# A score tile in PSUM with chunk 3 to the left of chunk 0, and two mask products at its head instead of three

## The chip, the cores and the metric

The kernel runs on one core of a Trainium2 chip. Its engines work side by side, each through its own queue in program order: TensorE (PE for its products, PEld for the loads of their weights), VectorE (DVE), ScalarE (ACT), GpSimd (POOL), and SyncE (SP), which issues most of the DMAs. The metric is the device time of one execution in microseconds (us); the profile gives one execution of its own with a span, from the first to the last instruction of the program.

## What is computed

Causal attention over 8 batches of 12 heads (448 positions, 64 per head), and on its output a soft mixture of experts with 8 experts of 4 slots each.

```python
scores = scale * np.matmul(q, k.transpose(0, 1, 3, 2))
mask = np.triu(np.ones((seq, seq), dtype=bool), k=1)
scores = np.where(mask, -1000000000.0, scores)
scores = scores - np.max(scores, axis=-1, keepdims=True)
attn = np.exp(scores)
attn = attn / (np.sum(attn, axis=-1, keepdims=True) + 1e-09)
out = np.matmul(attn, v)
...
logits = x @ phi
...
return (c @ slot_out).astype(np.float32)
```

## The kernel before

**Tiles.** Work goes head by head, i from 0 to 95 (`NHD`), two heads to a pair p. The scores of a head are held transposed: keys on the 128 partitions, queries along the columns. The keys are cut into four chunks of 128, 128, 128 and 64. Because of the causal mask, chunk c only meets queries from 128c on, so the chunks have 448, 320, 192 and 64 columns, 1024 in all: a tile `s` of two PSUM banks, of which three exist. Where each chunk lies is set by `SC0` to `SC3` (line 49): chunks 1 and 2 fill the first bank (columns 0 to 511), chunk 0 begins the second bank at 512 and chunk 3 ends it at 960.

**Products of a tile.** The first 128 columns of a chunk (64 for chunk 3) lie on the diagonal and need the mask. It is put there by TensorE: the weights are an identity in bf16 (`identb`) and the moving operand is `tri`, zeros with large negative numbers where a key is later than a query. `scores1(i, part)` (line 211) issues one product: `"c3"` and `"c0"` write the mask for chunks 3 and 0 (64 and 128 columns), `"c12"` that for chunks 1 and 2 in one product of 256 columns, since both lie in one bank; `"k0"` to `"k3"` add keys times queries (`ks` as weights, `qd` as moving operand). Each bank's first product carries `start`. Later `scores2` (`"t0"` to `"t3"`, line 285) adds the correction of the rounding and the row maxima, with `k2` as weights and `r2` as moving operand. Every product is preceded by a load of its weights; the weights of k0, k1 and k2 have 128 columns, those of k3 only 64.

**Readers of a tile.** `max_evac` (line 242) copies chunk 0 with ScalarE to `mx`, `max_keys` takes the maximum with chunks 1 to 3 on VectorE, `max_spread` puts the maxima into `r2` on GpSimd, `exps` (line 296) turns all 1024 columns into `pt`, and `attv` (line 300) multiplies it with the values: for each block qc of 128 queries a product for every chunk c up to qc, in f32, which the compiler makes two passes of. For qc = 3 only 64 queries are left and the weights have 65 columns, with one column more than needed; the last column of `pt` (1024) is a zero kept for this. The last head has a fresh PSUM tile, and there 128 columns are taken for c below 3.

**Order.** Each engine's order is written out by hand in `ORDER` (line 42), one list for even and one for odd i, and nothing is reordered. In round i the list issues the first products of head i + 2 (c, k), the corrections of head i (t), the value products of head i - 1 (a), the maxima (x, mr, sp), the norms (n), the casts and differences of coming pairs (ck, cq, sk, sq, c2), and at its end one item of a plan: transposes, logits or dispatch of a batch. Heads 0 to 3 get their first products in a row from `scores1_all` (line 238) before the rounds proper; heads 4 to 95 get them by `ORDER`.

**Start and tail.** Before the first scores, GpSimd makes `ident` and `tri` (line 153 on), and TensorE runs warm-up products with them. After the last head the experts run: 64 loads of 768 KB of weights, 22 of which go to buffers that are there from the start, the others to buffers that become free when attention ends.

Of the kernel before, what the change touches and what calls it, by code (L numbers as in the profile page):

```python
# [11 lines left out]
BF16 = mybir.dt.bfloat16  # L12
AF = mybir.ActivationFunctionType
ALU = mybir.AluOpType
# [3 lines left out]
P = 128  # L18
NB, NH, S, HD = 8, 12, 448, 64
# [10 lines left out]
NEG = -float(2 ** 33)  # L30
NHD = 2 * NPAIR
# [8 lines left out]


ORDER = (
# [4 lines left out]
)  # L47

SC0, SC1, SC2, SC3 = 512, 0, 320, 960
CQ0 = (0, 128, 256, 384)  # L50
SCOL = (SC0, SC1, SC2, SC3)

# [27 lines left out]
def attention_soft_moe(ctx: ExitStack, tc: tile.TileContext, qk, va, phi, w1, w2, out):  # L80
    nc = _Core(tc)
    const = ctx.enter_context(tc.tile_pool(name="const", bufs=1, side="left"))
# [29 lines left out]
    def load_qk(p, a, hs=slice(0, 2)):  # L112
        if p < NPAIR:
            if hs.start == 0:

                st["raw", a, p] = (wres.tile([P, WN], F32, tag="w", name=f"qk{a}_{p}")[:, 0:2 * S]
                                   .rearrange("p (h s) -> p h s", h=2)
                                   if (p, a) in ((1, 0), (2, 1)) else
                                   raw.tile([P, 2, S], F32, tag="qk", name=f"qk{a}_{p}"))
            nc.sync.dma_start(out=st["raw", a, p][:, hs], in_=qk[p, :, a, hs])  # L120

    def loads_v(p, eng=nc.sync):
        if p < NPAIR:
            eng.dma_start(out=va_[p % 2], in_=va[p])
# [12 lines left out]
    def load_w(n):  # L137
        if n < len(order):
            m, e, h, u = order[n]
            t = wtiles[order[n]] = slot(n, f"w{n}")  # L140
            nc.sync.dma_start(out=t, in_=(w1 if m == 0 else w2)[e, h, :, WN * u:WN * u + WN])

    for hs in (slice(0, 1), slice(1, 2)):
# [10 lines left out]
    nc.gpsimd.memset(ident, 0.0)  # L154
    nc.gpsimd.affine_select(out=ident, in_=ident, compare_op=ALU.not_equal, fill=1.0,
                            base=0, pattern=[[-1, P]], channel_multiplier=1)
    tri = const.tile([P, P], BF16, name="tri")
    nc.gpsimd.memset(tri, 0.0)
    nc.gpsimd.affine_select(out=tri, in_=tri, compare_op=ALU.is_ge, fill=NEG,
                            base=0, pattern=[[1, P]], channel_multiplier=-1)  # L160

    ops = [[fix.tile([P, 2, S], F32R, name=f"{o}{i}") for o in ("qd", "ks")] for i in range(NR)]
    qd_, ks_ = ([t[k] for t in ops] for k in range(2))
# [47 lines left out]
    def scores1(i, part):  # L211
        if i >= NHD:
            return
        p, h = divmod(i, 2)
        ks, qd = ks_[p % NR], qd_[p % NR]
        if ("s", i) not in st:
            st["s", i] = ps_s.tile([P, 1024], F32, tag="s", name=f"s{i}")
            st["open"] = set()
        s = st["s", i]

        bank = part in ("c12", "k1", "k2")
        start = bank not in st["open"]
        st["open"].add(bank)
        if part[0] == "k":
            c = int(part[1])
            w, m = S - CQ0[c], min(P, S - P * c)
            nc.tensor.matmul(s[0:m, SCOL[c]:SCOL[c] + w], ks[:, h, P * c:P * c + m],
                             qd[:, h, CQ0[c]:S], start=start, stop=False, skip_group_check=True)
            return
        if part == "c12":  # L230
            o = s[:, SC1:SC1 + 2 * SC2].rearrange("p (a n) -> p a n", n=SC2)[:, :, 0:P]
            mask = tri.unsqueeze(1).to_broadcast([P, 2, P])
        else:
            w = P if part == "c0" else S - 3 * P
            o, mask = s[:, SCOL[int(part[1])]:SCOL[int(part[1])] + w], tri[:, 0:w]
        nc.tensor.matmul(o, identb, mask, start=start, stop=False, skip_group_check=True)

    def scores1_all(i):
        for part in ("c0", "k3", "c3", "c12", "k2", "k1", "k0"):
            scores1(i, part)  # L240

    def max_evac(i):
        if i < NHD:
            st["mx", i] = (xtp.tile([P, 512], F32, tag="xt", name="mx1", bufs=2)[:, 0:S] if i == 1
                           else mx_)
            nc.scalar.activation(out=st["mx", i], in_=st["s", i][:, SC0:SC0 + S], func=AF.Copy)
# [38 lines left out]
    def scores2(i, cs):  # L285
        if i >= NHD:
            return
        p, h = divmod(i, 2)
        s = st["s", i]
        k2, r2 = k2_[p % NR], r2_[p % NR]  # L290
        for c in cs:
            w, m = S - CQ0[c], min(P, S - P * c)
            nc.tensor.matmul(s[0:m, SCOL[c]:SCOL[c] + w], k2[:, h, P * c:P * c + m],
                             r2[:, h, CQ0[c]:S], start=False, stop=True, skip_group_check=True)

    def exps(i):
        if i < NHD:
            nc.scalar.activation(out=pt_[i % 2][:, 0:1024], in_=st.pop(("s", i)), func=AF.Exp, scale=SCALE)

    def attv(i, qcs, first):  # L300
        if not 0 <= i < NHD:
            return
        p, h = divmod(i, 2)
        pt, v, po = pt_[i % 2], va_[p % 2], st.get(("po", i), po0)
        for qc in qcs:
            for c in range(qc + 1):
                col = SCOL[c] + P * (qc - c)


                m = P if qc < 3 or i == NHD - 1 and c < 3 else 65  # L310
                nc.tensor.matmul(po[0:m, qc], pt[:, col:col + m], v[:, c, h],
                                 start=c == 0 and qc in first, stop=c == qc, skip_group_check=True)

# [94 lines left out]
    for b in range(NB):  # L408
        o, last = 12 * b, b == NB - 1
# [14 lines left out]
    for hs in (h0, h1):  # L424
# [3 lines left out]
        sub_q(0, hs)  # L428
    scores1_all(0)
    scores1_all(1)  # L430
    warm(START[1])
    max_evac(0)
# [47 lines left out]
    for i in range(NHD + 1):  # L480
        p, h = divmod(i, 2)
        if h:
            load_qk(p + 3, 1)
            if p + 1 < NPAIR - 1:
                loads_v(p + 1)
            load_qk(p + 3, 0)
            if p % 2 and nload < RES:
                load_w(nload)
                nload += 1
        if i == NHD - 3:  # L490

            loads_v(NPAIR - 1, nc.scalar)
        if i < 2:
            scores2(i, (1, 0, 2))
            if i:
                scores1_all(3)
                max_evac(3)
            scores2(i, (3,))
            exps(i)
            if i == 0:  # L500
                max_row(1, 0)
                max_row(1, 1)
                max_spread(1)
                sub_q(1, h1)

        qs = [int(n[1]) for n in ORDER[h] if n[0] == "a"]
        first = qs[:2] if qs[0] == 3 else qs[:1]
        for n in ORDER[h]:
            if i < 2 and (n in ("ev", "exp") or n[0] in "kt" or n in ("c0", "c3", "c12")):
                continue  # L510
            if i == 0 and n in ("mr0", "mr1", "sp"):
                continue
            if n[0] == "k" or n in ("c0", "c3", "c12"):
                scores1(i + 2, n)
            elif n[0] == "t":
                scores2(i, (int(n[1]),))
            elif n[0] == "a":
                attv(i - 1, (int(n[1]),), first)
            elif n[0] == "x":
                max_keys(i + 2, int(n[1]))  # L520
            elif n[0] == "n":
                norm(i - 1, int(n[1]))
            elif n in ("mr0", "mr1"):
                max_row(i + 1, int(n[2]))
            elif n == "ld":
                if i % 12 == 3 and i > 12:
                    logits_d(i // 12 - 1, lt)
            elif n == "plan":
                if later and i:
                    later.pop(0)()  # L530
                plan.get(i, int)()
            else:
                {"ev": lambda: max_evac(i + 2), "exp": lambda: exps(i), "sp": lambda: max_spread(i + 1),
                 "ck": lambda: cast_k(p + 2), "sk": lambda: sub_k(p + 2), "cq": lambda: cast_q(p + 2),
                 "c2": lambda: copy_k2(p + 1), "sq": lambda: sub_q(p + 2)}[n]()
        if i == NHD - 1:

            scs.close()
            pe = att.enter_context(tc.tile_pool(name="pe", bufs=1, space=PSUM, reuse_waits="tile"))
            ps = [pe.tile([P, 512], F32, name=f"e{k}") for k in range(6)]  # L540
            po = st["po", i] = ps[2][:, 0:NCH * VC].rearrange("p (c n) -> p c n", n=VC)
# [44 lines left out]
    for hf in range(2):  # L586
        tps = (po0 if hf == 0 else po).rearrange("p a b->p (a b)")[:, 0:3 * NSLOT]
        for c in range(3):
            o = 384 * hf + P * c
# [130 lines left out]
    n = NBUF  # L720
# [80 lines left out]
```

## Time and profile before

| What | Value |
|---|---|
| three runs | 461.10, 459.82, 461.09 us |
| median | 461.09 us |
| profiled execution, its own time | 459.88 us |
| its span | 458.2 us |
| mean granted TensorE clock | 0.978 |
| HBM read, written | 107.25 MB, 11.01 MB |
| mask products (`s<-tri,identb`) | 288, busy 39.7 us, mean 234 ns |
| weight loads of `identb` | 320, mean 99 ns |

The span has two stages. Attention reaches to about 358 us and holds the 96 heads, at about 3.6 us each; in it GpSimd, VectorE, ScalarE and TensorE all work, and the DMA engines are about 70% busy. The rest are the experts, with the DMA engines full until close to the end. Rows of the profile give an engine, an operation, `out<-in` by the program's names, the shape, and a duration. For TensorE a product's duration is its way through the array, part of which overlaps with the next, so the pace is read from the distance between starts. All operations show line 64, that of a helper that records the program order, so they are told apart by their tiles.

### The profile page before, as it was taken

The numbers are of one execution on the slowest core, as the hardware profiler recorded it, in microseconds if no ns is written. First come the engines' busy times: TensorE is split into PE (matmuls) and PEld (weight loads), VectorE is DVE, ScalarE is ACT, GpSimd is POOL, SyncE is SP. The second block draws the span as 40 slices with busy tenths as digits, with TensorE's granted clock in tenths as the row PEclk, the third lists the DMA queues.
The fourth block names the chain that finished last, engine by engine and source line by source line (L and its number), as shares of the span: only waits on it lengthen the run. The fifth ranks groups of instructions, "written<-read, shape, count | busy, mean of one in ns | idle before, by whom it ended". The sixth has DMA issues, their size and how long they took to land.

```text
span 458.2 us, 12014 instructions
## 1 busy us (share of the span) xinstructions
PE 424.9 (93%) x4581; PEld 362.3 (79%) x4581; DVE 348.9 (76%) x1044; ACT 329.9 (72%) x496; POOL 266.3 (58%) x215
## 2 busy tenths in 40 slices
PE   6899999999999999999999999999999998996660
PEld 3798999999899989998999999999989654542230
DVE  6988888888888898888888888888886467332350
ACT  6898899889888988897899789988975211342240
POOL 5888777777777777777778777777771000000000
PEclk9999999999999999999999999999999999999875
DMA  7477666676667765777666766667758999999997
GB/s 267 128 259 243 235 193 224 216 239 223 204 208 237 236 221 171 241 241 231 210 188 225 254 222 216 191 213 253 231 160 300 369 411 415 414 414 413 402 391 284
DMA packets 38201, 119.04 MB, mean 260 GB/s; under 512 B 4096, under 2 KB 11776, under 8 KB 38144
## 3 DMA queue, kind: packets, MB, share of 16 engines
q1 hardware_dynamic: 38000, 118.01, 75.6%
q8 instruction: 36, 0.59, 0.5%
q10 hardware_dynamic: 144, 0.27, 0.2%
q14 instruction: 21, 0.17, 0.1%
HBM read 107.25 MB, written 11.01 MB: 258 GB/s over the span
## 4 chain that ended last, share of the span: by engine, by line
PE 77%; DMA 11%; POOL 5%; ACT 1%; DVE 1%; issue 1%; SPq 0%; POOLq 0%; ACTq 0%
PE po L64 34%; PE s L64 24%; DMA w<-in_w_dram 10%; PE xt L64 4%; PE g L64 3%; PE hp L64 3%; POOL r L64 3%; PE sp L64 2%; PE rt L64 2%; PE pp L64 2%; POOL ks L64 1%; PE e L64 1%; PE so L64 1%; DMA qk<-in_qk_dram 1%; ACT ot L64 0%
## 5 line engine op out<-in xcount | busy, mean ns | idle before, releaser
L64 PE MATMUL po<-va,pt 128*128 128x65 f32 x1900 | 193.6, 250 | 0.1
L64 PEld LDWEIGHTS po<-va,pt 128*128 128x128 f32 x1900 | 190.5, 171 | 0.5 <-issue 0.3
L64 DVE TENSOR_TENSOR mx<-s,mx 128x320 f32<-128x320 f32 (+2 forms) x288 | 100.8, 350 | 31.4 <-ACT mx L64 27.9
L64 POOL TENSOR_TENSOR r<-qk,qd 64x896 fp32r<-64x896 f32 (+1 forms) x50 | 101.5, 2030 | 6.5 <-ACT qd L64 2.7
L64 POOL TENSOR_SCALAR_AFFINE_SELECT r<-mr 14x448 fp32r<-14x448 f32 x96 | 61.4, 640 | 73.2 <-DVE mr L64 72.8
L64 ACT ACTIVATE pt<-s 128x1024 f32<-128x1024 f32 x96 | 98.2, 1023 | 6.3 <-PE s L64 3.1
L64 POOL TENSOR_TENSOR ks<-qk,ks 64x896 fp32r<-64x896 f32 (+1 forms) x47 | 98.1, 2087 | 4.5 <-ACT ks L64 0.9
L64 PE MATMUL s<-r,k 128*128 128x320 f32 (+3 forms) x384 | 83.2, 298 | 2.3 <-POOL r L64 2.2
L64 ACT ACTIVATE mx<-s 128x448 f32<-128x448 f32 x96 | 52.5, 546 | 36.0 <-PE s L64 22.2
L64 PE MATMUL s<-qd,ks 128*128 128x448 f32 (+3 forms) x384 | 76.0, 308 | 1.6 <-ACT qd L64 1.6
L64 PEld LDWEIGHTS s<-r,k 128*128 128x128 f32 (+1 forms) x384 | 60.0, 176 | 6.4 <-POOL r L64 2.9
L64 DVE STREAM_TRANSPOSE mt<-mx 128x448 f32<-128x448 f32 x96 | 61.9, 645 | 3.3
L64 DVE TENSOR_REDUCE r<-mt 128x14 f32<-128x448 f32 x96 | 58.4, 609 | 0.1
L64 PEld LDWEIGHTS s<-qd,ks 128*128 128x128 f32 (+1 forms) x384 | 55.0, 180 | 3.1 <-ACT qd L64 2.3
L64 ACT ACTIVATE ks<-qk 128x896 fp32r<-128x896 f32 (+1 forms) x50 | 45.6, 914 | 2.5 <-DMA qk<-in_qk_dram 2.5
L64 ACT ACTIVATE k<-ks 64x896 fp32r<-64x896 f32 (+1 forms) x49 | 45.8, 935 | 1.1
L64 ACT ACTIVATE qd<-qk 128x896 fp32r<-128x896 f32 (+1 forms) x50 | 46.1, 923 | 0.4 <-DMA qk<-in_qk_dram 0.3
L64 PEld LDWEIGHTS <-identb 128*128 128x128 bf16 x320 | 28.1, 99 | 20.1 <-issue 15.8
L64 DVE TENSOR_TENSOR x<-po,sm 128x256 f32<-128x256 f32 x95 | 40.3, 424 | 3.3
L64 PE MATMUL s<-tri,identb 128*128 128x64 bf16 (+2 forms) x288 | 39.7, 234 | 0.2
L64 ACT ACTIVATE xts<-xt 128x512 f32<-128x512 f32 x47 | 28.1, 598 | 6.7 <-PE xt L64 4.4
L64 PE MATMUL so<-w,ht 128*32 128x384 f32 x256 | 24.9, 492 | 7.4 <-DMA w<-in_w_dram 5.6
(124 smaller groups left out, 396.2 us busy)
## 6 DMA issues: line engine op xcount, KB each, us to landing
w<-in_w_dram SPq DMA_DIRECT2D x64, 768.0 KB, 7.5
qk<-in_qk_dram SPq DMA_DIRECT2D x94, 448.0 KB, 3.5
va<-in_va_dram SPq DMA_DIRECT2D x47, 260.0 KB, 3.5
out_dram<-ot SPq DMA_DIRECT2D x28, 384.0 KB, 6.5
qk<-in_qk_dram SPq DMA_DIRECT2D x4, 224.0 KB, 3.3
va<-in_va_dram ACTq DMA_DIRECT2D x1, 260.0 KB, 5.4
phi<-in_phi_dram SPq DMA_DIRECT2D x2, 48.0 KB, 3.9
```

What stands on the lines that cost most here:

```text
L64: return self._tc.keep_in_program_order(op(*args, **kwargs))
```

## The change

Chunk 3 moves to the head of the second bank (512), and chunk 0 behind it (576). The two diagonals of that bank are then neighbours, and one product of 192 columns, `"c03"`, writes both masks. Its moving operand is the new `tri3`, whose first 64 columns are the mask of chunk 3 and whose last 128 are the `tri` of before; GpSimd makes it with one memset and two selects. In both lists `"c03"` and `"c12"` stand first, and `"k3"` follows them; before it was `"c3", "c0", "k3", "c12"`. The order of `scores1_all` becomes `"c03", "k3", "c12", ...`.

Since it is now chunk 0 that ends the tile, its block for qc = 3 uses the zero column of `pt`. For the last head the value products of qc = 3 run in the order c = 1, 0, 2, 3, and only that of c = 1 takes 128 columns.

```diff
 ORDER = (
-    ("c3", "c0", "k3", "c12", "k1", "k0", "k2", "t0", "t2", "ev", "x1", "t1", "a0", "a3", "t3", "ck",
+    ("c03", "c12", "k3", "k1", "k0", "k2", "t0", "t2", "ev", "x1", "t1", "a0", "a3", "t3", "ck",
...
-    ("c3", "c0", "k3", "c12", "k0", "k1", "k2", "ev", "t0", "t1", "t2", "a0", "x0", "t3", "a3", "exp", "mr0",
+    ("c03", "c12", "k3", "k0", "k1", "k2", "ev", "t0", "t1", "t2", "a0", "x0", "t3", "a3", "exp", "mr0",
...
-SC0, SC1, SC2, SC3 = 512, 0, 320, 960
+SC0, SC1, SC2, SC3 = 576, 0, 320, 512
...
-    tri = const.tile([P, P], BF16, name="tri")
-    nc.gpsimd.memset(tri, 0.0)
-    nc.gpsimd.affine_select(out=tri, in_=tri, compare_op=ALU.is_ge, fill=NEG,
-                            base=0, pattern=[[1, P]], channel_multiplier=-1)
+    tri3 = const.tile([P, 64 + P], BF16, name="tri")
+    tri = tri3[:, 64:64 + P]
+    nc.gpsimd.memset(tri3, 0.0)
+    for t, n in ((tri3[:, 0:64], 64), (tri, P)):
+        nc.gpsimd.affine_select(out=t, in_=t, compare_op=ALU.is_ge, fill=NEG,
+                                base=0, pattern=[[1, n]], channel_multiplier=-1)
...
         else:
-            w = P if part == "c0" else S - 3 * P
-            o, mask = s[:, SCOL[int(part[1])]:SCOL[int(part[1])] + w], tri[:, 0:w]
+            o, mask = s[:, SC3:SC3 + 64 + P], tri3
         nc.tensor.matmul(o, identb, mask, start=start, stop=False, skip_group_check=True)

     def scores1_all(i):
-        for part in ("c0", "k3", "c3", "c12", "k2", "k1", "k0"):
+        for part in ("c03", "k3", "c12", "k2", "k1", "k0"):
             scores1(i, part)
...
         for qc in qcs:
-            for c in range(qc + 1):
+            last = qc == 3 and i == NHD - 1
+            for c in (1, 0, 2, 3) if last else range(qc + 1):
                 col = SCOL[c] + P * (qc - c)
-                m = P if qc < 3 or i == NHD - 1 and c < 3 else 65
+                m = P if qc < 3 or last and c == 1 else 65
```

More of the change, by code (lines that the diff above doesn't have):

```diff
@@ L508, in attention_soft_moe @@
         for n in ORDER[h]:
-            if i < 2 and (n in ("ev", "exp") or n[0] in "kt" or n in ("c0", "c3", "c12")):
+            if i < 2 and (n in ("ev", "exp") or n[0] in "kt" or n in ("c03", "c12")):
                 continue
@@ L512, in attention_soft_moe @@
                 continue
-            if n[0] == "k" or n in ("c0", "c3", "c12"):
+            if n[0] == "k" or n in ("c03", "c12"):
                 scores1(i + 2, n)
```

## The prediction

> **What bounds the kernel now.** I read the page first, for the shares of the engines and of the chain that ended last.
>
> ```profile
> span 458.2 us, 12014 instructions
> PE 424.9 (93%) x4581; PEld 362.3 (79%) x4581; DVE 348.9 (76%) x1044; ACT 329.9 (72%) x496; POOL 266.3 (58%) x215
> PE 77%; DMA 11%; POOL 5%; ACT 1%; DVE 1%; issue 1%; SPq 0%; POOLq 0%; ACTq 0%
> PE po L64 34%; PE s L64 24%; DMA w<-in_w_dram 10%; PE xt L64 4%; PE g L64 3%; PE hp L64 3%; POOL r L64 3%; PE sp L64 2%; PE rt L64 2%; PE pp L64 2%; POOL ks L64 1%; PE e L64 1%; PE so L64 1%; DMA qk<-in_qk_dram 1%; ACT ot L64 0%
> ```
>
> TensorE carries 77% of the chain, and its score products (s) and value products (po) carry 58%. Busy PE alone proves little, since the ends of products are modelled. So next come the busy time by stage, the waits from 39.4 to 346 us, and two places of the chain of waits.
>
> ```profile
> 39.40:346.00 306.60, 306.60 (x3364) 286.14 (x3365) 268.38 (x814) 266.55 (x380) 233.91 (x172) 1.00 0.70 219
> 362.00:458.20 96.20, 70.05 (x775) 35.62 (x774) 40.47 (x116) 23.74 (x61) 0.00 (x0) 0.90 1.00 394
> PEld L64 <- issue: 13.1, 36, 0.6
> PEld s L64 <- issue: 1.2, 7, 0.2
> PEld s L64 <- POOL r L64: 0.7, 1, 0.7
> 35.32 2.10 POOL ks L64
> 38.74 0.59 POOL r L64
> 39.38 0.72 PE s L64 x3
> ```
>
> The columns of the first two rows are the stretch, its length, PE, PEld, DVE, ACT and POOL busy, the granted clock, the DMA share and GB/s. From 39.4 to 346 us the next busiest engine after TensorE (DVE, 268.38) has 38 us to spare, the clock is full, and TensorE waits for another engine for at most 1.2 + 0.7 us; the 13.1 us are treated with the rivals. Up to 39.38 the chain runs through POOL, whose r ends TensorE's last long wait. From 362 us the DMA engines are full: that tail begins when attention frees its buffers, so attention's delay moves it.
>
> **The price of a product is read from the order of weight loads and streams.** Here is one score tile (starts first, then durations).
>
> ```profile
> 204.10 0.21 PEld L64 LDWEIGHTS <-identb 128*128 128x128 bf16 x2
> 204.21 0.25 PE L64 MATMUL s<-tri,identb 128*128 128x64 bf16 x2
> 204.24 0.14 PEld L64 LDWEIGHTS s<-qd,ks 128*64 128x64 f32 x1
> 204.27 0.22 PE L64 MATMUL s<-qd,ks 128*64 128x64 f32 x1
> 204.33 0.10 PEld L64 LDWEIGHTS <-identb 128*128 128x128 bf16 x1
> 204.33 0.28 PE L64 MATMUL s<-tri,identb 128*128 128x256 bf16 x1
> 204.33 0.20 PEld L64 LDWEIGHTS s<-qd,ks 128*128 128x128 f32 x1
> 204.46 0.34 PEld L64 LDWEIGHTS s<-qd,ks 128*128 128x128 f32 x2
> 204.60 0.45 PE L64 MATMUL s<-qd,ks 128*128 128x448 f32 x2
> 204.80 0.25 PE L64 MATMUL s<-qd,ks 128*128 128x192 f32 x1
> 204.81 0.19 PEld L64 LDWEIGHTS s<-r,k 128*128 128x128 f32 x1
> 204.91 0.39 PEld L64 LDWEIGHTS s<-r,k 128*128 128x128 f32 x2
> 202.07 0.55 PEld L64 LDWEIGHTS po<-va,pt 128*65 128x65 f32 x8
> 202.60 1.20 PEld L64 LDWEIGHTS po<-va,pt 128*128 128x128 f32 x10
> 202.71 1.23 PE L64 MATMUL po<-va,pt 128*128 128x65 f32 x10
> 7.96 0.61 PE L64 MATMUL warm<-tri,identb 128*128 128x512 bf16 x2
> 7.96 0.82 PE L64 MATMUL warm<-tri,identb 128*128 128x512 bf16 x3
> ```
>
> Prices, worked out:
>
> - A bf16 stream: a third 512-column product adds 0.82 - 0.61 = 0.21 us, or 0.41 ns a column.
> - A score stream: k0 (448 columns) starts at 204.60 and k2 at 204.80: 0.20 us, or 0.45 ns a column.
> - A load of 128 f32 columns: ten loads start over 1.20 - 0.19 us, so (1.20 - 0.19) / 9 = 0.112 us. Their products stream only 65 columns (0.03 us) and still come 0.11 us apart, so here the loads set the pace.
> - A load of 65 columns: (0.55 - 0.14) / 7 = 0.059 us; I take it for 64 too.
>
> The order: one load runs ahead, no more. The second of the two loads at 204.46 (k2's) starts when the product before it does, at 204.60 (0.46 + 0.34 - 0.19 = 0.61), though the load before it was through at 204.57. The r load at 204.81 starts with k2's product, and the next at 204.91, when that 0.1 us load is through. So a load is hidden as far as the product ahead of it streams, and the rest is idle time.
>
> In this kernel the long mask product c12 (256 columns, 0.105 us) hides the 0.112 us load of the key product k1. From c3's start to k1's: k0 starts at 204.60, less k1's 320 columns (0.143 us) gives 204.46, which is also where k0's load begins. So **0.25 us** before.
>
> **The change part by part.**
>
> *The two mask products merged and moved.* c3 (64 columns) and c0 (128) become c03 (192 columns); one bf16 load and one product go from each of 96 tiles. Since c12 now follows at once, the order is c03, c12, k3, k1 (k0 on odd heads). c03 streams 192 x 0.41 = 0.079 us and hides c12's load; c12 streams 0.105 us and hides k3's load of 0.059 us. Then k3 streams its 64 columns (0.029 us) and has to cover the 128-column load of k1, which starts when k3 does: 0.112 us. So 0.079 + 0.105 + 0.112 = **0.296 us** from the first mask to k1, against 0.25: **+0.046 us a tile**. What is late next is k1 and all behind it, since TensorE takes its queue in order. The mask moved ahead of k3 waits for the same tile to come free as c03 just before it, so no new wait is added, and no DMA or other queue is moved.
>
> No row of before has a 64-column score product followed by a 128-column f32 load, so the bounds: below, the load is hidden wholly, 0.079 + 0.105 + 0.029 = 0.213 us, or -0.037 a tile; above, the load starts only when k3's stream has ended, as c12's did (k3 starts at 204.24 + 0.06 = 204.30, c12's load at 204.33), 0.029 later, or +0.075 a tile. I take +0.046, the rule of the po loads, which are the nearest rows: a 65-column f32 stream ahead of a 128-column f32 load.
>
> The queue speaks for the low bound in one text: the Trainium skill, "TensorE: Matmul & The Clock Gate", table at its head, gives TensorE a 64-deep window that pulls weight loads ahead of products in flight. Taken as many loads ahead, it would make this change a gain, and the rows at 204.46 and 204.81 speak against it.
>
> How many tiles count:
>
> ```profile
> L64 PE MATMUL s<-tri,identb 128*128 128x256 bf16 x85 | 24.3, 285 | 0.0
> 66.96 0.95 ACT L64 ACTIVATE k<-ks 64x896 fp32r<-64x896 f32 x1
> 68.03 0.50 PEld L64 LDWEIGHTS s<-r,k 128*128 128x128 f32 x3 [0.17 <-issue]
> ```
>
> Of the 96 tiles, 85 lie between 39.4 and 346 us: 85 x 0.046 = 3.9 us. The seven in ORDER before 39.4 I cost at nothing, because POOL sets the pace there and TensorE waits for it anyway; without that cover 7 x 0.046 = 0.3 us. Seven waits (1.2 us) are like the one at 68.03, where ACT's copy k ends at 66.96 + 0.95 = 67.91 and TensorE stands 0.17 us: the later scores use up 0.046 of each, 7 x 0.046 = -0.3 us.
>
> *Start.* POOL gets a wider memset and one more select ahead of the warm-up.
>
> ```profile
> 1.58 0.29 POOL L64 TENSOR_SCALAR_AFFINE_SELECT tri<-tri 128x128 bf16<-128x128 bf16 x1
> 4.75 0.13 PEld L64 LDWEIGHTS s<-qd,ks 128*64 128x64 f32 x1 [0.59 <-ACT qd L64]
> 7.11 0.53 ACT L64 ACTIVATE mx<-s 128x448 f32<-128x448 f32 x1
> ```
>
> Some 0.3 us, after which the first scores end near 6 us instead of 5.7, while their reader, the copy mx, starts at 7.11: 0, and 0.3 without that cover. The first four tiles keep k3 ahead of c12 and lose one product, at a time when DMA and POOL set the pace: 0.
>
> *Last head.* Two of its value products, two passes each, load 65 columns instead of 128.
>
> ```profile
> L64 PEld LDWEIGHTS e<-va,pt 128*128 128x128 f32 x18 | 2.2, 192 | 0.2 <-issue 0.2
> ```
>
> 4 x (0.112 - 0.059) = -0.21 us, behind which the full DMA tail stands: 0, or -0.2 if that cover is gone.
>
> *Sum:* 3.9 - 0.3 = **+3.6 us**. The profiled execution took 459.88 us, so 463.5 by it. The median of the runs is 461.09, as two of the three lie near 461.1 and one at 459.8; +3.6 on it is 464.7. I put down **464.3**.
>
> **The rivals.**
>
> 1. *The load waits for k3 to end* (+0.075 a tile). For it: the late load at 204.33. Against it: the same step from a 64-column score product to the po loads, where the load at 202.07 is not late.
>
> ```profile
> 202.01 0.14 PEld L64 LDWEIGHTS s<-r,k 128*64 128x64 f32 x1
> ```
>
> 202.01 + 0.06 = 202.07. Price: 85 x 0.075 = 6.4, less 0.5 for the seven waits, plus 0.3 for the tiles before 39.4: +6.2 on the median, 467.3. The Trainium skill, "TensorEngine Tiling (Array Packing)", Key Properties, says that a change of tiling mode drains TensorE. By that rule k3's 64 columns would cost this wait; the two rows disagree about it. Chance 0.14.
>
> 2. *Faster: the load is hidden.* If TensorE keeps more than one load ready, k1's load runs under c12 beside k3's (0.059 + 0.112 = 0.171 us against 0.079 + 0.105 streamed), and only the missing waits remain: 85 x -0.037 = -3.1 on the median, or 458.0. It decides as soon as 0.046 us of the load starts before k3 does. The loads at 204.46 and 204.81 speak against it. Chance 0.12.
>
> 3. *No change:* TensorE has slack that no view names. The 36 waits of 13.1 us in front of mask loads would be such slack in 36 tiles; I read them as loads held back by long streams ahead (the logits and dispatch products). With them as slack, and a load hidden in part in the rest, the time stays near 461. Against it: 1.2 + 0.7 us are all the waits that name an engine or a queue on score loads, and 3.9 are needed. Chance 0.12.
>
> **How the numbers follow.** The forecast has 0.62. About 0.3% (1.4 us) is what a measurement of this kernel tells from no change. Slower: 0.62 + 0.14 = 0.76; same 0.12; faster 0.12. The range takes in rival 1 up to 467.3, and stops below at 460.2, which leaves out rival 2 and a little of rival 3.
>
> **What would show it.** Right: one mask form of 192 columns x96; k1's product some 0.30 us after the first mask of its tile, with the load of k1 starting beside k3 and the next load 0.11 us later; the stretch of 85 tiles longer by 3 to 4 us, and the DMA tail moved by as much. Wrong: k1's load under c12 (rival 2), k1's load 0.03 us after k3's start (rival 1), or a stretch no longer than before (rival 3). I would also be wrong if the moved layout made the copies or the exponential dearer, which no row suggests.

## The result

| | before | changed |
|---|---|---|
| median of six runs each | 461.10 us | 465.46 us |
| lowest, highest | 459.66, 463.04 | 465.02, 466.93 |
| profiled execution, span | 459.88, 458.2 | 465.78, 464.1 |

The ratio is 1.0103, with a 95% interval of 1.0072 to 1.0133: slower by 0.7 to 1.3%, as forecast, with 464.3 predicted and 465.46 measured. The profiled executions of the first and the seventh run below took 1416.37 and 621.32 us, with TensorE at a slow pace throughout, so those two kernels were run again for their profiles.

First the page of the changed kernel, then its two stretches from the view by windows: from the c12 product of head 11 to that of head 95, and the rest. The columns are the stretch, its length, PE, PEld, DVE, ACT and POOL busy, the clock, the DMA share and GB/s.

```profile
span 464.1 us, 11824 instructions
PE 431.1 (93%) x4485; PEld 367.7 (79%) x4485; DVE 348.7 (75%) x1044; ACT 330.0 (71%) x496; POOL 266.4 (57%) x216
L64 PE MATMUL s<-tri,identb 128*128 128x192 bf16 x96 | 24.2, 252 | 0.2
L64 PEld LDWEIGHTS <-identb 128*128 128x128 bf16 x224 | 19.4, 102 | 21.4 <-issue 17.9 <-DVE identb L64 1.7
```

```profile
44.54:352.29 307.75, 307.61 (x3236) 287.71 (x3236) 265.44 (x806) 264.15 (x377) 230.85 (x170) 1.00 0.69 215
352.29:464.00 111.71, 85.09 (x938) 48.57 (x937) 48.32 (x143) 31.06 (x73) 1.28 (x2) 0.93 0.99 389
```

The same two stretches of the kernel before:

```profile
42.59:345.81 303.22, 303.22 (x3322) 283.04 (x3320) 265.69 (x806) 263.79 (x377) 230.87 (x170) 1.00 0.69 218
345.81:458.20 112.39, 85.89 (x939) 49.16 (x937) 48.39 (x143) 31.12 (x73) 1.28 (x2) 0.91 0.99 386
```

The change does what it says: 96 products of 192 columns, and 96 loads of `identb` fewer (224 instead of 320). With them TensorE takes **307.75 us instead of 303.22** for the same 84 steps from tile to tile, 4.5 us more with less work. The other engines' busy time is the same. The rest of this pair of executions (+2.0 us ahead of head 11; 111.78 against 112.36, so -0.6 us, from head 95 to the last instruction) is taken up under the start alone and under the last head.

Where most of the 4.5 us come from is seen in one tile, which stands at the same place of the kernel as the one in the prediction. The timeline of the changed kernel:

```profile
208.75 0.36 PE L64 MATMUL s<-tri,identb 128*128 128x192 bf16 x2
208.84 0.27 PE L64 MATMUL s<-tri,identb 128*128 128x256 bf16 x1
208.84 0.14 PEld L64 LDWEIGHTS s<-qd,ks 128*64 128x64 f32 x1
208.87 0.28 PE L64 MATMUL s<-qd,ks 128*64 128x64 f32 x1
208.95 0.30 PEld L64 LDWEIGHTS s<-qd,ks 128*128 128x128 f32 x2
209.06 0.34 PEld L64 LDWEIGHTS s<-qd,ks 128*128 128x128 f32 x2
209.20 0.36 PE L64 MATMUL s<-qd,ks 128*128 128x448 f32 x1
```

From the first mask to k0 it takes 209.20 - 208.75 = 0.45 us, where it took 204.60 - 204.21 = 0.39. The load of k3 starts with c12's stream (208.84) and is hidden. The load of k1, the first of the two at 208.95, starts when c12's stream is over and k3's begins, and the next load follows 0.11 us later, at 209.06: that is the whole load, with only k3's 0.03 us of stream above it. In the kernel before, k1's load started at 204.33 with c12's stream as its cover.

One of the 84 steps holds something else as well. Just ahead of this very tile (head 56) TensorE stood idle, because a transfer of q and k came late. ACT's copy qd waited for it, and what comes behind that copy on ACT, VectorE and TensorE was late too:

```profile
205.12 0.95 ACT L64 ACTIVATE qd<-qk 128x896 fp32r<-128x896 f32 x1 [0.30 <-DMA qk<-in_qk_dram]
208.26 0.42 PEld L64 LDWEIGHTS xt<-ident,x 128*128 128x128 f32 x4 [0.28 <-DVE mr L64]
```

The kernel before has no such wait in its stretch. Compared step by step, from one c12 start to the next, this step (head 55 to 56) grew by 0.40 us. Seven steps grew by 0.02 us together, and the other 76 by 0.054 us on the mean (0.035 to 0.070). Those 76 make 4.1 of the 4.5 us.

### The profile page after: what moved, and what is told of

The parts are those of the page before. It is cut to its first block, busy times and chain, and to the rows that moved or that the text cites. A ratio compares the mean times of both kernels' runs of the same rounds, so it can differ in the third digit from the quotient of the medians.

```text
span 464.1 us, 11824 instructions
## 1 busy us (share of the span) xinstructions
PE 431.1 (93%) x4485; PEld 367.7 (79%) x4485; DVE 348.7 (75%) x1044; ACT 330.0 (71%) x496; POOL 266.4 (57%) x216
## 4 chain that ended last, share of the span: by engine, by line
PE 65%; DMA 11%; POOL 9%; DVE 4%; ACT 3%; issue 3%; SPq 0%; POOLq 0%; DVEq 0%; ACTq 0%
PE po L64 28%; PE s L64 21%; DMA w<-in_w_dram 6%; POOL r L64 5%; PE xt L64 4%; DMA qk<-in_qk_dram 3%; POOL ks L64 3%; PE g L64 2%; PE sp L64 2%; PE rt L64 2%; DMA out_dram<-ot 2%; DVE lm L64 1%; PE pp L64 1%; PE e L64 1%; PE hp L64 1%
## 5 line engine op out<-in xcount | busy, mean ns | idle before, releaser
L64 PE MATMUL s<-qd,ks 128*128 128x448 f32 (+3 forms) x384 | 77.3, 323 | 1.1 <-ACT qd L64 1.1
L64 PEld LDWEIGHTS s<-qd,ks 128*128 128x128 f32 (+1 forms) x384 | 56.0, 179 | 2.5 <-ACT qd L64 1.8
L64 PEld LDWEIGHTS <-identb 128*128 128x128 bf16 x224 | 19.4, 102 | 21.4 <-issue 17.9
L64 PE MATMUL s<-tri,identb 128*128 128x192 bf16 x192 | 35.4, 264 | 0.2
```

Of the source, the lines that this page charges most:

```text
L64: return self._tc.keep_in_program_order(op(*args, **kwargs))
```

## The experiments

The theory: a weight load is hidden only by the stream of the one product ahead of it, and the change put the shortest product, k3, where the longest mask product had been. The rivals: the new layout or the wider mask costs, the step from bf16 masks to f32 products costs, the change from one PSUM bank to the other costs, or the start does.

**k3 put back between the masks** (first and fifth run, the same kernel)

```diff
-    ("c03", "c12", "k3", "k1", ...
+    ("c03", "k3", "c12", "k1", ...
-    ("c03", "c12", "k3", "k0", ...
+    ("c03", "k3", "c12", "k0", ...
```

> The changed kernel with k3 put back between the two mask products (c03, k3, c12, k1); layout and merged mask stay. Theory (the load of k1 lost its cover): c12 covers k1's load again; from the first mask to k1 0.082 + 0.052 + 0.109 = 0.243 us, as in the kernel before (0.246), so the time falls back to 460.5 to 461.5 us. Rival (the layout or the 192-column mask is what costs): it stays near 465.5.

> The same kernel as e1_k3_between, for a profile at full clock and a narrower interval. Theory: from head 11 to head 95 the stretch is within 0.5 us of the 303.2 us of the kernel before; the product k3 starts as c03's stream ends, c12's load starts as k3's stream ends, k1's load starts under c12. Time 459.5 to 461. Rival (the first 45 us carry a cost of the wider mask): the stretch is equal, but the time 1 to 2 us above the kernel before.

Measured: 460.12 us against 460.68 (ratio 0.9983, 0.9963 to 1.0003), and again 459.69 against 461.00 (0.9969, 0.9952 to 0.9985). The second set's timeline, and the stretch from head 11 to head 95:

```profile
204.11 0.25 PE L64 MATMUL s<-tri,identb 128*128 128x192 bf16 x1
204.12 0.14 PEld L64 LDWEIGHTS s<-qd,ks 128*64 128x64 f32 x1
204.14 0.25 PE L64 MATMUL s<-qd,ks 128*64 128x64 f32 x1
204.22 0.10 PEld L64 LDWEIGHTS <-identb 128*128 128x128 bf16 x1
204.23 0.21 PEld L64 LDWEIGHTS s<-qd,ks 128*128 128x128 f32 x1
204.36 0.34 PEld L64 LDWEIGHTS s<-qd,ks 128*128 128x128 f32 x2
```

```profile
42.77:345.53 302.76, 302.76 (x3236) 282.60 (x3236) 265.65 (x806) 264.01 (x377) 231.00 (x170) 1.00 0.69 218
```

The load of the product after k1 starts when k1's stream does, so k1 starts at 204.36, 0.25 us after the first mask at 204.11; 0.243 was expected. k1's load (204.23) is under c12 again. With layout, wide mask and start of the changed kernel kept, the whole loss is gone, so none of these is its cause. The second set says a little faster than the kernel before, by 0.15 to 0.5%; the profile shows 0.46 us (0.1%) of that in the stretch, and where the rest would lie it does not show.

**The order alone, in the kernel before** (old layout, three masks)

```diff
-    ("c3", "c0", "k3", "c12", ...
+    ("c3", "c0", "c12", "k3", ...
```

(in both lists)

> The kernel before, layout and three masks kept, with only the order changed to c3, c0, c12, k3. Theory: k3 alone stands ahead of k1's load, 0.029 + 0.056 + 0.109 + 0.111 = 0.305 us against 0.246, so +4.5 to +5 us, about 466, and no extra us in the start. Rival (layout or merged mask): 461, as before.

Measured: 465.53 us, ratio 1.0107 (1.0075 to 1.0138). Its timeline, and the stretch:

```profile
202.82 0.19 PE L64 MATMUL s<-tri,identb 128*128 128x64 bf16 x1
202.91 0.30 PEld L64 LDWEIGHTS s<-qd,ks 128*64 128x64 f32 x2
203.02 0.30 PEld L64 LDWEIGHTS s<-qd,ks 128*128 128x128 f32 x2
```

```profile
42.64:353.37 310.73, 309.33 (x3320) 289.30 (x3320) 265.73 (x806) 264.27 (x377) 230.75 (x170) 0.99 0.68 213
```

The load behind k1's starts at 203.02 + 0.30 - 0.19 = 203.13, and k1 with it: 0.31 us after the first mask, where 0.305 was expected. The loss comes without the layout and without the merged mask. The stretch of this execution (467.18 us, one of the two longest of the six) is longer than the order explains. Two of its steps, heads 19 to 21, grew by 3.5 us: qd waits 1.75 us for a transfer of q and k, TensorE stands, and its granted clock is 0.59 and 0.56 from 76 to 78 and from 78 to 80 us. The other 82 steps grew by 4.0 us.

**k3 one place later**

```diff
-    ("c03", "c12", "k3", "k1", "k0", "k2", ...
+    ("c03", "c12", "k1", "k3", "k0", "k2", ...
-    ("c03", "c12", "k3", "k0", "k1", "k2", ...
+    ("c03", "c12", "k0", "k3", "k1", "k2", ...
```

> The changed kernel with k3 one place later: c03, c12, k1, k3, k0 (odd heads c03, c12, k0, k3, k1). Theory: any 128-column load behind k3 is uncovered; now it is that of the third product, so the time stays at 465 to 466, with the late product one place later in the trace. Rival (what costs is the step from the bf16 masks to the f32 products, not k3's shortness): the step c12 to k1 is then that of the kernel before, and the time 461.

Measured: 465.74 us, ratio 1.0107 (1.0070 to 1.0144). The load behind k3 in one tile, and the stretch by the view by windows:

```profile
200.97 0.30 PEld L64 LDWEIGHTS s<-qd,ks 128*128 128x128 f32 x2
```

```profile
43.67:351.22 307.55, 307.55 (x3235) 285.17 (x3236) 265.63 (x806) 264.11 (x377) 230.82 (x170) 1.00 0.68 215
```

307.55 us, as in the changed kernel, though a mask product is followed directly by a 128-column f32 load here, as in the kernel before. So it is not the step from masks to f32 products; it is what stands behind k3. There k0's load starts with k3 (200.97) and the next one only when it is through, at 200.97 + 0.30 - 0.19 = 201.08. No late transfer lies in this stretch: its 84 steps grew by 4.3 us.

No run was made for the rival of the banks, but the lists of the changed kernel speak against it. c0, c3, k0 and k3 write the second bank, c12, k1 and k2 the first. The even list now changes banks five times from the first mask to k2, where it changed three times before; the odd list changes three times in both kernels. Yet from the first mask to the first wide product's stream both take the same: 0.307 us on the mean in the even tiles and 0.308 in the odd ones, against 0.248 and 0.249 before.

**k3 behind the other three** (seventh run, and once more for its profile)

```diff
-    ("c03", "c12", "k3", "k1", "k0", "k2", ...
+    ("c03", "c12", "k1", "k0", "k2", "k3", ...
-    ("c03", "c12", "k3", "k0", "k1", "k2", ...
+    ("c03", "c12", "k0", "k1", "k2", "k3", ...
```

> The changed kernel with k3 behind the other three (c03, c12, k1, k0, k2, k3; odd heads k0, k1, k2, k3). Theory, by load and stream: k3's load is hidden under k2 (0.087), and the r load behind k3 is uncovered (0.111); but the r load was already 0.025 uncovered behind k2, so a tile costs 0.082 + 0.109 + 0.087 + 0.111 = 0.389 against 0.246 + 0.111 = 0.357 of the kernel before: +0.032 a tile, stretch 84 x 0.032 = 2.7 us longer, less some 0.2 at the seven waits: 463 to 463.5. Rival (a 64-column product costs a fixed 0.054 ahead of any 128-column load): 465.5.

> The same kernel as e7_k3_last, for a profile at full clock. Theory: k3's load starts with k2's stream and is through before it ends; the load behind k3 starts with k3 and the r product follows 0.11 us after k3's start; the stretch from head 11 to head 95 takes 303.2 + 84 x 0.032 - 0.2 = 305.7 us. Rival (a fixed 0.054 a tile): 307.7, as in the changed kernel.

Measured: 463.45 us, ratio 1.0043 (1.0021 to 1.0066); the second run is one execution, 462.49 us against 461.87. Its timeline, and the stretch by windows:

```profile
202.85 0.13 PEld L64 LDWEIGHTS s<-qd,ks 128*64 128x64 f32 x1
202.94 0.19 PEld L64 LDWEIGHTS s<-r,k 128*128 128x128 f32 x1
202.97 0.60 PE L64 MATMUL s<-r,k 128*128 128x448 f32 x2
```

```profile
42.86:348.58 305.72, 305.72 (x3235) 286.19 (x3235) 266.64 (x806) 263.83 (x377) 230.93 (x170) 1.00 0.68 216
```

This run could have broken the theory. The product is the same and a 128-column load follows it as before, yet the stretch is longer by 305.72 - 303.22 = 2.50 us only, where 2.5 had been worked out (84 x 0.032 - 0.2). k3's load ends under k2, and the r load starts with k3, at 202.94. The r load that now stands behind k3 was already short of cover behind k2, so less is lost. A fixed price for a short product would have given 307.7.

**k3's weights 65 columns wide, between the masks**

```diff
+            kw = ks[:, h, P * c:P * c + m]
+            if c == 3 and i > 3:
+                m, o = 65, S * h + P * c
+                kw = ksf_[p % NR][:, o:o + m]
-            nc.tensor.matmul(s[0:m, SCOL[c]:SCOL[c] + w], ks[:, h, P * c:P * c + m],
+            nc.tensor.matmul(s[0:m, SCOL[c]:SCOL[c] + w], kw,
```

(`ksf_` is the same buffer seen flat, with four columns of zeros behind it; the order is that of the first experiment.)

> As e1_k3_between, but from head 4 on k3's weights have 65 columns instead of 64 (one row more of chunk 3 is written, which meets zero values). If c12's load stands 0.03 us late behind k3 because 64 columns are another tiling mode of TensorE, that wait goes: 0.028 less in each of 92 tiles, 458.5 to 459.5, faster than both kernels. If it is late because bf16 weights follow an f32 product, nothing changes against e1: 460.5 to 461.5.

Measured: 460.66 us, ratio 0.9994 (0.9972 to 1.0016). Its timeline:

```profile
203.14 0.24 PE L64 MATMUL s<-tri,identb 128*128 128x192 bf16 x1
203.14 0.13 PEld L64 LDWEIGHTS s<-qd,ks 128*65 128x65 f32 x1
203.24 0.10 PEld L64 LDWEIGHTS <-identb 128*128 128x128 bf16 x1
```

The `identb` load still starts 0.10 us after k3's load, as at 204.12 and 204.22 with 64 columns. So 64 columns are not what makes that load late.

**The start alone, in the kernel before**

```diff
-    tri = const.tile([P, P], BF16, name="tri")
-    nc.gpsimd.memset(tri, 0.0)
...
+    tri3 = const.tile([P, 64 + P], BF16, name="tri")
+    tri = tri3[:, 64:64 + P]
+    nc.gpsimd.memset(tri3, 0.0)
...
```

(with the two selects of the changed kernel)

> The kernel before with only the start of the changed one: GpSimd makes the 192-column mask with a memset and two selects, and the three masks are taken from it. Predicted theory (the start is hidden): 460 to 461.5, no difference that can be measured, the first c12 some 0.1 us later. Rival (the later start costs what the profile of the changed kernel shows up to head 11, some 2 us): 462 to 463.

Measured: 460.64 us against 461.00, ratio 0.9991 (0.9971 to 1.0011). From its waits, ahead of the first product:

```profile
PE warm L64 <- POOL tri L64: 2.2, 1, 2.2
```

The warm-up starts 0.3 us later than before (2.2 us instead of 1.9), as worked out, and the time doesn't change. So the 2.0 us by which the profiled execution of the changed kernel reached head 11 late (44.54 against 42.59 us) are not the price of the start. Its chain shows two transfers of q and k there:

```profile
2.20 4.72 DMA qk<-in_qk_dram
25.11 4.97 DMA qk<-in_qk_dram
```

In the kernel before, the first such piece of the chain lasts 4.41 us and there is none at 25 us. The fifth run, with the same start, has its head 11 at 42.77 us and the sixth at 42.68. The profile of the order alone, with the loss in it, reaches head 11 at 42.64, so heads 4 to 10 show no price of the order either, as the prediction had it. That leaves the late transfers as the likely cause; with one profile of each kernel it is not shown.

## Why the prediction was right, step by step

**The bound** was right. In the 84 steps TensorE sets the pace, but for the late transfers; each change of its order moved the other steps by about what loads and streams gave.

**The merge and the move** had the right mechanism and a size too small. Predicted was 0.296 us from the first mask to k1 against 0.25, measured is 209.06 - 208.75 = 0.31 against 204.46 - 204.21 = 0.25, and by k0's start 0.45 against 0.39: +0.06 instead of +0.046. In the trace's nanoseconds it is 303 against 245. The term that was mis-sized is the streams, which were priced without anything per product: c12 starts 83 ns behind c03 (79 priced), and k1's load starts 110 ns behind c12 (105 priced). The load behind k3 was priced rightly at 112 (110 measured). Together these make 7 ns. The other 5 lie in the 0.25 of before: k1's stream, taken off k0's start as 143 ns, lasts 147, and 249 was rounded to 250.

**The bounds of the load behind k3.** It starts with k3 (208.95), neither under c12 nor 0.03 us later. That was the rule of the po loads, and rivals 1 and 2 fall with this row. Of the Trainium skill's two statements, the window that pulls loads ahead ("TensorE: Matmul & The Clock Gate", table at its head) reaches one load in the score and value products of these runs. It is not one load everywhere: with sp, whose weights have 32 columns, all eight loads start within 0.16 - 0.11 = 0.05 us, 0.11 being the length of one, while the last four products only begin at 207.67 and after. These are rows of the kernel before:

```profile
207.32 0.16 PEld L64 LDWEIGHTS sp<-x,gs 128*32 128x32 f32 x8
207.32 0.85 PE L64 MATMUL sp<-x,gs 128*32 128x384 f32 x8
```

The drain at a change of tiling mode ("TensorEngine Tiling (Array Packing)", Key Properties) is not seen behind k3 at 208.95.

**The waits on ACT's copy** were used up by as much as the scores came later, as predicted. In the stretch of the changed kernel the view of waits has no row left of score loads waiting for issue, where seven waits of 1.2 us had been. Here is the tile whose wait the prediction showed at 68.03:

```profile
69.72 0.56 PEld L64 LDWEIGHTS s<-qd,ks 128*64 128x64 f32 x4
70.38 0.50 PEld L64 LDWEIGHTS s<-r,k 128*128 128x128 f32 x3
```

The loads ahead of the r load end at 69.72 + 0.56 = 70.28, and it starts at 70.38: 0.10 us are left of the 0.17, too short for the view to list. The seven steps with these waits are the ones that grew by 0.02 us together.

**The count.** Predicted were 3.9 - 0.3 = 3.6 us, and 3 to 4 us as the sign of being right; the stretch grew by 4.5. Of that, 0.4 is the step with the late transfer, which is not the order's but for some 0.05 of it, and 76 x 0.054 = 4.1 are the steps that only the order changed. The rest of the difference is the term of one tile, 0.054 a step instead of 0.046. Why a step grows by 4 ns less than its tile (58 ns) was not looked into.

**The start** at nothing: right, by the run of the start alone. **The last head** at nothing, behind the full DMA tail: no gain is to be seen. Its loads went from 18 of 128 columns to 14. From the c12 product of head 95 to the end, the runs with the old last head took 112.36 us (the kernel before), 112.08 and 111.94, those with the new one 111.78 (the changed kernel), 112.28, 112.42, 112.03 and 112.19: 112.1 on the mean in both groups.

**Rival 3**, slack that no view names, falls: the stretch grew. The 36 waits in front of mask loads were no slack; the changed kernel still has them. In both kernels 22 of them stand behind the logits products (g) and 14 behind the dispatch products (sp), as the prediction read them: the load starts 0.20 and 0.41 us after the last of these products does.

```profile
PEld L64 <- issue: 13.1, 36, 0.6
```

## What to carry to other kernels

Where TensorE sets the pace, price a move by pairs, the load of each product against the stream of the product ahead of it; a product and a load taken away can cost time if the neighbours change. In these runs it paid to put the short product where a short load follows it, and to keep a long stream ahead of a 128-column f32 load. Look at single steps too before a sum is compared with a forecast: one late transfer was 0.4 us of the 4.5 here. The merged mask with k3 left between the two mask products (459.69 against 461.00 us) is the version to keep.

## What the runs showed of the hardware that was not expected

A bf16 load of `identb` behind k3 does not start with k3's stream but at its end. It starts at 204.22, with c03 begun at 204.11 and streaming 0.08 us: k3 begins at 204.19, and the load 0.03 us later, which is k3's stream. It was the same with weights of 65 columns (203.24 behind 203.14). An f32 load behind k3 starts with it (208.95), and so does an f32 load behind a bf16 mask (k3's own at 208.84).

This is no rule for every f32 product. Behind the transposes xt, f32 as well, the `identb` load of the changed kernel's tile starts with the last product:

```profile
208.54 0.14 PEld L64 LDWEIGHTS xt<-ident,x 128*128 128x128 f32 x1
208.65 0.10 PEld L64 LDWEIGHTS <-identb 128*128 128x128 bf16 x1
```

The last load of xt starts at 208.54 and takes 0.11 us, so its product begins at 208.65, as the `identb` load does; it is so behind all 44 groups of xt ahead of a mask. Why the load waits behind k3 was not settled; it is the reason why k3 between the masks isn't free.
